# Gated linear attention, spectral mixing and a gated convolution: another way to form the next state, and an earlier place for a weight piece

## The chip, the cores and the metric

The kernel runs on one core of a Trainium2 chip. The metric is device time in microseconds (us) of one execution; three executions of the kernel before took 575.1, 575.26 and 575.69 us. The core has five engines with a queue each: PE (TensorE, matrix products; its weight loads are shown apart as PEld), DVE (VectorE), ACT (ScalarE), POOL (GpSimd) and SP (which issues the DMAs here). Each queue runs in order.

## The reference

```
# 1: gated linear attention, per batch (4), head (8), time step (768), head size 48
state = alpha[t][:, None] * state + outer(k[t], v[t])
y[t]  = q[t] @ state
# 2: spectral mixing, x = y as (4, 768, 384)
theta = x @ w_theta
zr, zi = x * cos(theta), x * sin(theta)
u = x + w_tok_r @ zr + w_tok_i @ zi          # w_tok: 768 x 768, over time
x = u + relu(u @ w_ch)
# 3: gated convolution
h = relu(x @ w_in)                           # 384 -> 1024
c = conv over time, kernel 3, of h
out = (h * sigmoid(c)) @ w_out
```

## The kernel before, in words

**Chunks.** The sequence is cut into chunks of 128 time steps, six to a batch (NC), 24 in all (NCH). Within a chunk the recurrence is done by matrix products. `a_prep` forms running products of alpha by two scans on DVE (L245, L250) and multiplies q and k by them (L259); `ftot` holds, for each of the 4 pairs of heads and each of the 2 x 48 state rows, the chunk's total decay (copied by ACT, L253), and ACT reads both scans once more to guard against overflow (the `Square` of L256, which writes into the tile that the alphas came in and reads the scan's tile, of which there is one). `a_score` makes the masked scores: matmuls into `sc`, copies by ACT to `pt` (L277), the causal mask on POOL (L278); it also turns k into `kt` (transposes L268, copy L282). `a_y` adds the chunk's own part (scores times v) and the old state's part (q times S) into `y` on PE, copies `y` to `x` on ACT (L302), and makes the next state. `a_xt` turns x (L336) and copies it to `u` (L337); `a_theta` does the sine and cosine part and splits its result into a high part `zh` (ACT cast) and a low part `zl` (DVE).

**State.** Two tiles S of 128 x 4 x 96 take turns. Rows 0 to 47 and 64 to 111 are the two heads of a pair, the third dimension has 48 columns for each; only the two diagonal blocks of 48 x 48 for a pair are non-zero. The state is kept already multiplied by the next chunk's decay, so that S for chunk c+1 is (S of c plus k^T v of c) times `ftot` of c+1. In the kernel before, PE makes `kv` for both heads of a pair at once (96 columns, of which half are not used, L308), DVE adds S and kv (L312), and POOL multiplies the two blocks by the decay (L320, twice). In the first chunk of a batch there is no old state: ACT copies the two blocks of kv (L317) and POOL multiplies.

**Token weights.** `w_tok` comes in 12 pieces of 128 x 2 x 384 words of 8 bytes (`load_tok`, `load_split`): a DMA into one of two staging buffers (STB), a decode of three DVE instructions (L116 to L118), and then, later, in `piece()`, a cast on ACT (L73) and the low part on DVE (L74), after which the staging buffer is free for another DMA. The cast is tied by an order-only edge (`behind`) to come after the latest pt, kt, x and u copies issued so far.

**Order.** A planner orders each engine's queue at build time from a simulated run; what comes earlier in the program goes first where two are ready. `a_att(b, c)` loads two chunks ahead, preps and scores one chunk ahead, then does `a_y` and `a_xt` of its own chunk. In batch 0 `piece()` follows `a_att`, in the loop of b = 0 too, for the second half of the token weights. The token mixing of batch b (`m_mix`: 18 matmuls for a chunk into `yps`) runs on PE among the attention of batch b + 1, and in batch 0 as its inputs come ready. After the four batches, parts 2 and 3 go on with PE as the busiest engine.

## Time and profile before

| | |
|---|---|
| median of three executions | 575.26 us |
| the profiled execution's own time | 576.95 us |
| its span, first to last instruction | 575.2 us |
| busy PE / PEld | 552.1 us (96%) / 523.4 us (91%) |
| busy DVE / ACT / POOL | 452.5 (79%) / 335.3 (58%) / 94.5 us (16%) |
| chain that ended last | PE 75%, DVE 13%, DMA 4%, POOL 3%, ACT 2%, issue 2% |

The span is the time between the first and the last instruction of the profiled execution; its own time has 1.75 us more around it. A table by stretch shows how long each engine was busy in it, and the clock that PE was granted as a share of full speed. A row of the timeline has the start, the duration, the engine, the line, the operation and its tiles, and in brackets how long the engine had sat idle just before and what released it.

### The profile page before, as it was taken

The page shows a single profiled execution, that of the slowest core. Times are in us where ns is not written, and L with a number is a line of the kernel's source. Part 1 is how long each engine was busy: PE and PEld are TensorE (multiplying, and loading weights), DVE is VectorE, ACT ScalarE, POOL GpSimd, SP SyncE. Part 2 cuts the span into 40 slices and gives each one's busy share as a digit, 9 for nine tenths or more (in the row PEclk, how much of TensorE's full clock was granted, in tenths as well). Part 3 has the DMA queues.
Part 4 walks back from the last instruction along what each step waited for, and adds up shares of the span by engine and source line. Part 5 has one row for each costly group of instructions (what it writes and reads, how often), then busy time and mean ns, then how long its engine had stood idle before and what let it go on. Part 6 is the DMA issues. An engine that isn't in the chain of part 4 may idle for free.

```text
span 575.2 us, 10883 instructions
## 1 busy us (share of the span) xinstructions
PE 552.1 (96%) x4371; PEld 523.4 (91%) x4371; DVE 452.5 (79%) x682; ACT 335.3 (58%) x685; POOL 94.5 (16%) x99
## 2 busy tenths in 40 slices
PE   6887988999999999999999999999999999999996
PEld 3776877887899999999999999999999999999996
DVE  8899997999866775551657989997888889798781
ACT  3576664546864467542742435557766776667571
POOL 2455415540044300350000000000000000000000
PEclk9599999999999999999999999999999999999999
DMA  8556642764034400310005333221043445536001
GB/s 326 148 180 192 206 147 73 248 215 172 15 94 138 170 2 14 95 60 2 1 2 188 113 111 111 82 83 42 15 144 136 173 138 167 193 107 229 20 30 46
DMA packets 25402, 66.59 MB, mean 116 GB/s; under 512 B 2560, under 2 KB 8704, under 8 KB 24960
## 3 DMA queue, kind: packets, MB, share of 16 engines
q1 hardware_dynamic: 25344, 65.82, 34.4%
q8 instruction: 36, 0.59, 0.4%
q14 instruction: 22, 0.18, 0.1%
HBM read 61.10 MB, written 4.72 MB: 114 GB/s over the span
## 4 chain that ended last, share of the span: by engine, by line
PE 75%; DVE 13%; DMA 4%; POOL 3%; ACT 2%; issue 2%; SPq 0%; DVEq 0%; ACTq 0%; POOLq 0%
PE yps L65 22%; PE ops L65 17%; PE hps L65 15%; PE th L65 5%; PE y L65 5%; PE cps L65 3%; PE sc L65 3%; PE kv L65 2%; DMA stage<-in_w_tok_dram 2%; POOL S L320 2%; DVE fbt L245 1%; PE xps L336 1%; DMA stage<-in_w_out_dram 1%; POOL pt L278 1%; DVE stage L117 1%
## 5 line engine op out<-in xcount | busy, mean ns | idle before, releaser
L65 PE MATMUL yps<-wtok,zh 128*128 128x384 f32 x576 | 152.7, 343 | 1.3 <-ACT zh L73 1.3
L65 PEld LDWEIGHTS yps<-wtok,zh 128*128 128x128 f32 x576 | 104.3, 189 | 4.7 <-ACT zh L73 1.6
L65 PE MATMUL hps<-x,win 128*128 128x386 f32 x576 | 107.3, 339 | 0.0
L65 PE MATMUL ops<-wout,g 128*128 128x384 f32 x576 | 107.1, 338 | 0.0
L65 PEld LDWEIGHTS hps<-x,win 128*128 128x128 f32 x576 | 102.1, 189 | 0.0
L65 PEld LDWEIGHTS ops<-wout,g 128*128 128x128 f32 x576 | 101.7, 187 | 0.0
L65 PE MATMUL yps<-wtok,zl 128*128 128x384 f32 x288 | 96.8, 340 | 0.3 <-DVE zl L74 0.3
L278 POOL TENSOR_SCALAR_AFFINE_SELECT pt<-pt 128x512 f32<-128x512 f32 x48 | 59.0, 1252 | 151.6 <-ACT pt L277 151.5
L65 PEld LDWEIGHTS yps<-wtok,zl 128*128 128x128 f32 x288 | 54.4, 189 | 1.6 <-DVE zl L74 0.6
L245 DVE TENSOR_TENSOR_SCAN fbt<-a_t,onehot 128x516 f32<-128x516 f32 x24 | 29.8, 1242 | 24.7 <-ACT a_t L256 22.9
L74 DVE TENSOR_TENSOR g<-cv,g 128x384 fp32r<-128x384 f32 x64 | 35.5, 555 | 15.0 <-ACT g L73 14.4
L550 ACT ACTIVATE cv<-cv 128x384 f32<-128x384 f32 x64 | 33.2, 522 | 22.5 <-DVE cv L547 22.5
L544 DVE SCALAR_TENSOR_TENSOR cv<-hh,cw,cv 128x383 f32<-128x383 f32 (+1 forms) x64 | 38.5, 615 | 7.3 <-ACT cv L541 6.9
L73 ACT CAST g<-cv 128x384 fp32r<-128x384 f32 x64 | 32.6, 510 | 15.3 <-DVE cv L551 13.9
L551 DVE SCALAR_TENSOR_TENSOR cv<-cv,hh 128x384 f32<-128x384 f32 x64 | 35.2, 556 | 7.7 <-ACT cv L550 5.9
L541 ACT ACTIVATE cv<-hh,cw 128x384 f32<-128x384 f32 x64 | 38.4, 615 | 4.2 <-DVE g L74 3.9
L65 PE MATMUL cps<-us,wch 128*128 128x384 f32 x216 | 40.2, 338 | 0.2 <-DVE u L495 0.2
L547 DVE SCALAR_TENSOR_TENSOR cv<-hh,cw,cv 128x384 f32<-128x384 f32 (+1 forms) x64 | 38.3, 615 | 0.6
L65 PEld LDWEIGHTS cps<-us,wch 128*128 128x128 f32 x216 | 38.1, 188 | 0.5 <-issue 0.5
L539 ACT ACTIVATE hh<-hps 128x386 f32<-128x386 f32 x64 | 31.4, 492 | 9.8 <-PE hps L65 9.6
L368 DVE TENSOR_TENSOR zf<-x,zf 128x768 f32<-128x768 f32 x24 | 23.8, 992 | 13.1 <-ACT zf L367 13.1
L259 DVE TENSOR_TENSOR qk_t<-qk_t,fbt 128x1024 f32<-128x1024 f32 x24 | 32.8, 1365 | 0.9
(90 smaller groups left out, 828.5 us busy)
## 6 DMA issues: line engine op xcount, KB each, us to landing
qk_t<-in_qka_dram SPq DMA_DIRECT2D x24, 512.0 KB, 4.6
stage<-in_w_tok_dram SPq DMA_DIRECT2D x12, 768.0 KB, 4.7
top<-in_w_tok_dram SPq DMA_DIRECT2D x12, 768.0 KB, 4.3
a_t<-in_qka_dram SPq DMA_DIRECT2D x24, 260.0 KB, 2.7
v_t<-in_v_dram SPq DMA_DIRECT2D x24, 192.0 KB, 3.8
out_dram<-ob SPq DMA_DIRECT2D x24, 192.0 KB, 1.9
stage<-in_w_in_dram SPq DMA_DIRECT2D x4, 768.0 KB, 4.4
stage<-in_w_out_dram SPq DMA_DIRECT2D x4, 768.0 KB, 4.3
```

The lines of the kernel that those rows point to most:

```text
L65: nc.tensor.matmul(o, lhsT, rhs, start=start, stop=stop, skip_group_check=True)
L73: cast = nc.scalar.copy(hi, src)
L74: lo_eng.tensor_tensor(lo, src, hi.bitcast(F32), ALU.subtract)
L245: nc.vector.tensor_tensor_scan(bf[:, AW:0:-1], at[:, AW:0:-1], of[:, AW:0:-1], 0.0, ALU.mult, ALU.add)
L259: nc.vector.tensor_tensor(q4, q4, fl.rearrange("p b (a t) -> p b a t", a=4)[:, :, :, :P], ALU.mult)
L278: nc.gpsimd.affine_select(pt, pt, [[0, NP], [1, P]], ALU.is_ge, 0.0, base=0, channel_multiplier=-1)
L539: nc.scalar.activation(hh, ps[:, :HW], AF.Relu)
L541: nc.scalar.activation(cv, hh[:, o : o + HALF], AF.Copy, scale=cw[:, f, 1:2])
L544: nc.vector.scalar_tensor_tensor(cv[:, a:HALF], hh[:, o + a - 1 : o + HALF - 1], cw[:, f, 0:1], cv[:, a:HALF], ALU.mult, ALU.add)
L547: nc.vector.scalar_tensor_tensor(cv[:, 0:e], hh[:, o + 1 : o + 1 + e], cw[:, f, 2:3], cv[:, 0:e], ALU.mult, ALU.add)
L550: nc.scalar.activation(cv, cv, AF.Tanh, scale=0.5)
L551: nc.vector.scalar_tensor_tensor(cv, cv, 1.0, hh[:, o : o + HALF], ALU.add, ALU.mult)
```

## The change

The next state is formed by other engines, in another order. POOL multiplies the old state by the decay (before kv is needed), ACT scales kv by the same decay as it reads it from PSUM (one instruction for each pair, 48 columns), and DVE adds the two, a block at a time. In the first chunk of a batch ACT writes the scaled blocks straight into the new state: eight instructions, and POOL has none. PE makes kv for each head by itself, 48 columns to a matmul, in as many matmuls as before. And `piece()` is called in `a_att` between the scores of the next chunk and `a_y` of this one, in place of after `a_att`.

```diff
-                    kv = ps_a.tile([P, NP, 2 * D], F32, tag="a", name="kv")
+                    kv = ps_a.tile([P, NP, D], F32, tag="a", name="kv")
                     for p in range(NP):
-                        for t in halves:
-                            mm(kv[t, p, :], kt[:, p, t], vt[:, p * 96 : p * 96 + 96], p == 0, True)
+                        for j, t in enumerate(halves):
+                            h = 2 * p + j
+                            mm(kv[t, p, :], kt[:, p, t], vt[:, h * D : (h + 1) * D], p == 0, True)
                     nft = prep[ci + 1][2]
+                    blocks = [(slice(64 * j, 64 * j + D), slice(j * D, (j + 1) * D)) for j in range(2)]
                     if c > 0:
-                        tt = att.tile([P, NP, 2 * D], F32, tag="tst", name="tst", bufs=1)
-                        nc.vector.tensor_tensor(tt[:112], Sp[:112], kv[:112], ALU.add)
+                        tt = att.tile([P, 2, NP, D], F32, tag="tst", name="tst", bufs=1)
+                        for r, e in blocks:
+                            nc.gpsimd.tensor_tensor(
+                                tt[r, 0], Sp[r, :, e], nft[r].unsqueeze(2).to_broadcast([D, NP, D]), ALU.mult
+                            )
+                        for p in range(NP):
+                            nc.scalar.activation(tt[:112, 1, p], kv[:112, p], AF.Copy, scale=nft[:112, p : p + 1])
+                        for r, e in blocks:
+                            nc.vector.tensor_tensor(Sn[r, :, e], tt[r, 0], tt[r, 1], ALU.add)
                     else:
-                        tt = Sn
-                        for j in range(2):
-                            nc.scalar.copy(Sn[r, :, j * D : (j + 1) * D], kv[r, :, j * D : (j + 1) * D])
-                    for j in range(2):
-                        nc.gpsimd.tensor_tensor(Sn[r, ...], tt[r, ...], nft[r] broadcast, ALU.mult)
+                        for p in range(NP):
+                            for r, e in blocks:
+                                nc.scalar.activation(Sn[r, p, e], kv[r, p], AF.Copy, scale=nft[r, p : p + 1])
...
-            def a_att(b, c):
+            def a_att(b, c, between=None):
...
                     a_prep(ci + 1)
                     a_score(ci + 1)
+                if between:
+                    between()
                 a_y(ci)
                 a_xt(ci)
...
             for c in range(NC):
-                a_att(0, c)
+                a_att(0, c, None if slow or c == 0 else piece)
...
-                else:
+                elif slow:
                     piece()
                 piece = load_tok(0, c)
...
-                    a_att(b + 1, c)
+                    a_att(b + 1, c, None if slow or b > 0 or c == 0 else piece)
                     if b == 0:
-                        if c > 0:
+                        if slow and c > 0:
                             piece()
                         piece = load_tok(1, c)
```

## Rows read from the trace of the kernel before

**Rows 1.** Busy time by stretch: stretch, length, PE, PEld, DVE, ACT, POOL, PEclk, DMA, GB/s.
```profile
40.00:60.00 20.00, 16.16 (x195) 13.96 (x195) 19.42 (x24) 12.75 (x26) 13.40 (x8) 0.92 0.59 179
60.00:80.00 20.00, 20.00 (x184) 16.76 (x185) 19.48 (x23) 12.92 (x25) 4.63 (x5) 1.00 0.53 180
80.00:100.00 20.00, 16.38 (x214) 14.46 (x211) 15.80 (x21) 11.38 (x23) 10.74 (x8) 1.00 0.28 90
160.00:200.00 40.00, 40.00 (x526) 37.79 (x525) 26.77 (x32) 20.32 (x47) 18.06 (x20) 1.00 0.45 141
```

**Rows 2.** Waits of PE over the whole span: waiter, released by: us in total, times, longest.
```profile
PE y L65 <- POOL S L320: 6.0, 4, 2.3
PE yps L65 <- ACT zh L73: 1.3, 1, 1.3
```

**Rows 3.** Timeline, PE: old-state part of y, three of the four waits.
```profile
45.03 0.88 PE L65 MATMUL y<-S,qk_t 128*64 128x96 f32 x16 [1.51 <-POOL S L320]
55.62 0.88 PE L65 MATMUL y<-S,qk_t 128*64 128x96 f32 x16 [2.33 <-POOL S L320]
92.38 0.88 PE L65 MATMUL y<-S,qk_t 128*64 128x96 f32 x16 [1.96 <-POOL S L320]
```

**Rows 4.** Timeline, batch 1: first chunk's state, copied by ACT, multiplied by POOL.
```profile
83.84 5.51 POOL L278 TENSOR_SCALAR_AFFINE_SELECT pt<-pt 128x512 f32<-128x512 f32 x2 [13.23 <-ACT pt L277]
85.91 0.66 ACT L317 COPY S<-kv 48x192 f32<-48x192 f32 x2
89.32 3.01 POOL L320 TENSOR_TENSOR S<-S,ftot 48x192 f32<-48x192 f32 x2
```

**Rows 5.** Chain that ended last, in order of time: start, us, what.
```profile
154.31 1.07 PE y L65 x32
170.96 0.66 PE kv L65 x16
```

**Rows 6.** Instructions that touch S: duration ns min/median/max.
```profile
L320 POOL TENSOR_TENSOR S<-tst,ftot x32: 498/504/3965, 30.8 to 259.2; 48x192 f32<-48x192 f32 x32
L312 DVE TENSOR_TENSOR tst<-S,kv x16: 532/541/555, 29.7 to 258.0; 112x384 f32<-112x384 f32 x16
L317 ACT COPY S<-kv x8: 310/314/320, 17.6 to 230.5; 48x192 f32<-48x192 f32 x8
```

**Rows 7.** Groups of instructions by shape, 0 to 270 us: busy us, mean ns.
```profile
L253 ACT COPY ftot<-fbt 128x4 f32<-128x4 f32 x24 | 4.8, 198 | 41.3 <-DVE fbt L245 31.8 <-POOL S L320 9.5
L249 DVE RECIPROCAL starts<-fbt 128x4 f32<-128x4 f32 x24 | 4.3, 178 | 0.6
L74 DVE TENSOR_TENSOR wth<-stage,wth 128x768 fp32r<-128x768 f32 x1 | 1.0, 952 | 0.0
L74 DVE TENSOR_TENSOR wth<-stage,wth 128x384 fp32r<-128x384 f32 x1 | 0.6, 551 | 0.0
```

**Rows 8.** The page's groups: ACT with and without a scale read from a tile.
```profile
L73 ACT CAST g<-cv 128x384 fp32r<-128x384 f32 x64 | 32.6, 510 | 15.3 <-DVE cv L551 13.9
L541 ACT ACTIVATE cv<-hh,cw 128x384 f32<-128x384 f32 x64 | 38.4, 615 | 4.2 <-DVE g L74 3.9
```

**Rows 9.** Timeline, batch 0: ACT's Square and the scans of DVE behind it.
```profile
23.17 1.23 DVE L245 TENSOR_TENSOR_SCAN fbt<-a_t,onehot 128x516 f32<-128x516 f32 x1 [1.41 <-ACT a_t L256]
31.77 0.19 ACT L256 ACTIVATION_READ_ACCUMULATOR a_t<-fbt 128x1 f32 x1
32.08 1.53 DVE L245 TENSOR_TENSOR_SCAN fbt<-a_t,onehot 128x516 f32<-128x516 f32 x1
51.52 0.20 ACT L256 ACTIVATION_READ_ACCUMULATOR a_t<-fbt 128x1 f32 x1
53.47 1.21 DVE L245 TENSOR_TENSOR_SCAN fbt<-a_t,onehot 128x516 f32<-128x516 f32 x1
```

**Rows 10.** Timeline, batch 0, a later chunk: state, piece and staging buffer.
```profile
48.60 0.56 DVE L116 TENSOR_SCALAR stage<-stage 128x768 uint32<-128x768 uint32 x1 [0.41 <-DMA stage<-in_w_tok_dram]
49.45 0.48 ACT L337 COPY u<-xps 128x384 f32<-128x384 f32 x1
```

## What was predicted before the run

> **What bounds the kernel now.** The table by stretch comes first, because the change touches only the attention part (the first 265 us) and the bound there is not the same throughout. From 160 to 200 us PE is busy for the whole 40 us while DVE works 26.8 and ACT 20.3: there PE is the bound, and the next state is formed in its shadow. From 40 to 60 us PE has 16.2 of 20 us and DVE 19.4; from 60 to 80 both are full (PE 20.0, DVE 19.5); from 80 to 100 both have holes (16.4 and 15.8) [rows 1]. So the early stretch is held by DVE and by chains that pass through it, and in the late one each PE instruction saved is time saved.
>
> The waits of PE come next. Its largest is the old-state part of y waiting for POOL to write S: 6.0 us in four waits [rows 2]. The timeline has three of them: 1.51 us at 45.0 and 2.33 us at 55.6, in batch 0, and 1.96 us at 92.4, behind the first chunk of batch 1 [rows 3]; what is left over, 0.2 us, is the fourth. The instructions that touch S say why: a multiply by POOL takes 504 ns in the middle of the list and 3,965 ns at the longest [rows 6]. The reader should see that the change aims at these four waits and at the width of kv, and that the first two lie where DVE, not POOL, has no time left.
>
> **The change part by part.**
>
> *kv with 48 columns.* There are as many matmuls, half as wide. The trace has the same form in the chunk's own part of y: 32 records in 1.07 us, 33.4 ns each, against 16 records of kv in 0.66 us, 41.3 ns each [rows 5]. So a chunk's kv falls from 0.66 to 0.53 us, by 0.13 us. Fifteen chunks make kv from batch 1 on, where PE is the bound: 15 x 0.13 = 2.0 us gained. The five in batch 0 give nothing while DVE holds the pace. Bounds: nothing, if weight loads set the pace of either width, and half of 0.66, 15 x 0.33 = 5.0 us, if columns alone did. I take 2.0, since the narrow form itself is in the rows.
>
> The Trainium skill (TensorE: Matmul & The Clock Gate, section Back-to-back issue gap) gives an isolated matmul of up to 64 columns a floor of about 25 ns. By that a record of kv would fall by 16 ns rather than 8, and this term would be an estimated 3.9 us. The 33.4 ns of the trace, in a stream with a weight load for each matmul, speak for the smaller figure.
>
> *The first chunk of a batch.* Now: two copies by ACT, 0.66 us, then POOL, whose two multiplies took 3.01 us at 89.3 because they stood behind two masks of together 5.51 us [rows 4]. After: eight ACT instructions of 48 columns with the scale read from a tile, and no POOL. No row has this form. A copy of 4 columns takes 198 ns [rows 7], one of 192 columns 314 ns [rows 6], so 48 columns lie near 225 ns; a scale read from a tile adds 615 - 510 = 105 ns [rows 8]: 0.33 us each. Bounds: 0.20 (the small copy) and 0.42 (192 columns plus the scale). Eight are 2.64 us, 1.98 more than the copies (0.94 to 2.7). At 85.9 us this puts S at about 88.6 in place of 92.3, before the mask that y waits for anyway (83.84 + 5.51 = 89.35) [rows 4]. The wait of 1.96 us at 92.4 goes, and as DVE has holes there, I count it in full: with the 0.2 us of the fourth wait 2.2 us gained. What is late next is the mask on POOL, then PE's own queue.
>
> *The later chunks.* L312 on DVE (541 ns) and POOL's multiplies behind it give way to four ACT instructions (4 x 0.33 = 1.32 us, 0.8 to 1.7) and two adds of 192 columns on DVE; POOL's multiplies stay, 32 of them, but read the old S and need not wait for kv. An add costs, by the line through 551 ns (384 columns) and 952 ns (768) [rows 7], 0.35 us; two are 0.70, 0.16 more than L312. Bounds for one are 178 ns (the smallest DVE row there [rows 7]) and L312's 541: -0.2 to +0.5 us a chunk. In batches 1 to 3 PE covers this, and ACT too, with half of its time free [rows 1]. The path from kv to S was L312 and two multiplies, at least 0.54 + 2 x 0.50 = 1.54 us [rows 6], and is now 1.32 + 0.70 = 2.02 us; PE, full from 160 to 200 us with the mixing between the chunks, never waited for the old one, so I cost the 0.5 us at nothing. Without that cover it would be 12 x 0.5 = 6 us.
>
> *Batch 0, where nothing covers.* Each chunk's new ACT work stands in ACT's queue ahead of the Square, and the next scan of DVE (L245) must wait for the Square, since it overwrites the scans' tile. At 23.2 us DVE already sat 1.41 us for it; at 32.08 the scan began 0.12 us after the Square's read-out ended (31.96); at 53.47 there are 1.75 us between them [rows 9]. So the first chunk's 1.98 us can fall on DVE; I take 1.0, half, because a ready decode instruction can be planned into that hole. The second chunk's 1.32 us falls where slack is 0.1: I take 0.7, half again, as the add and the piece may go in between. The third and fourth have slack like that at 53.5, over 1.32: nothing. The last one's ACT work meets an ACT that waits for PE, nothing. The adds give 4 x 0.16 = 0.6. Sum: 2.3 us more for DVE.
>
> Two waits of 3.84 us in all leave PE in this batch [rows 3]. They are worth nothing by themselves as long as DVE has 19.4 us of work in 20: PE would then wait for a scan, a z or a piece instead.
>
> *The piece.* Cast and low part move ahead of x and u of the same chunk. In ACT's queue that frees the cast from one copy of 0.48 us (u), not more, since it stays tied behind pt and kt. Its DMA waits for the buffer that the low part frees, so the next DMA can start by up to 0.48 us sooner; DVE waited 0.41 us for such a DMA at 48.6 [rows 10]. SP's queue gets no new issue, only these earlier; the loads queued behind it move by as much. The low part of 0.95 us (the 768-column row [rows 7]) may now be planned ahead of the adds, which delays S by so much: PE has no need of S so soon. I take 0.4 us gained for one such wait, bounds 0.95 lost and 1.0 gained.
>
> Batch 0 then has DVE 1.9 us later. Part of DVE's work there (scans two chunks ahead, decodes for the second half of the weights) has time to spare, so I count half: 0.9 us lost.
>
> **Sum.** -2.0 - 2.2 + 0.9 = -3.3 us. The profiled execution goes from 576.95 to 573.65 us, its span from 575.2 to 571.9. The median of the runs, 575.26, lies 1.69 below that execution; I take the same difference: 572.0 us.
>
> **The rivals.**
>
> *PE, not DVE, sets batch 0.* Then the first two waits pay as well, and DVE's 2.3 us lie in slack. For it: PE is full from 60 to 80 us. Against it: DVE is as well [rows 1]. Time: 575.26 - 2.0 - 6.0 = 567.3 us.
>
> *ACT takes POOL's place: slower.* If the planner puts every scaled copy ahead of the Square, L245 starts late in each chunk of batch 0: 1.98 + 4 x 1.32 = 7.3 us, less the 4.2 gained, is 3.1 us slower, 578.3 us. It decides from the point at which the added ACT time exceeds the gap between Square and scan, 0.1 us in one row and 1.75 in the other [rows 9]. For it: PE, DVE and ACT hang in one loop there. Against it: ACT works 12.8 of 20 us [rows 1] and loses 9.5 us of waits of `ftot` for POOL [rows 7], which the early multiply frees.
>
> *The add comes as late as POOL did.* DVE's queue, not POOL, decides when S is ready, and the wait at 92.4 stays in another name. Then only kv's width is left, less the 0.9: 575.26 - 1.1 = 574.2, no change. Against it: DVE has holes at that place.
>
> *DVE and POOL shut each other out.* The long POOL multiplies show that POOL slows beside a busy DVE [rows 6]; L312 reads one operand from PSUM, the new adds read both from SBUF, and so can be caught in turn. If each of the eight adds of batch 0 is 0.3 us longer (as the scan that took 1.53 us in place of 1.21 [rows 9]), 2.4 us go: 574.4, no change. The Trainium skill (SBUF — State Buffer, section Who interferes with whom) states it as a rule: a DVE instruction with two SBUF inputs contends with a POOL instruction that reads SBUF. By that rule each add is at risk; the stretched multiplies agree that the two meet, and no row has an add of this kind.
>
> **How the numbers follow.** The forecast has a chance of 0.40, PE as the bound in batch 0 0.18, ACT in POOL's place 0.20, the late add 0.16, the shut-out 0.06. Less than 0.2% (1.15 us) is no change that a measurement of this kernel can tell. The forecast's own range is 569.5 to 574.5, so nearly all of it, and the first rival, are faster: with a little of the others 0.60. The two in the middle give 0.20, ACT's rival 0.20 slower. The range goes from 567.0, the first rival, to 577.8, most of ACT's.
>
> **What would show it.** kv as 16 records in about 0.53 us in the chain; no wait of PE for S at the first chunk of batch 1, and S there by ACT before the mask ends; ACT instructions of 0.33 us; in batch 0 DVE no less full, with a wait of L245 for the Square longer than 1.41 us near 23 us, and PE waiting for something else than POOL. The prediction is wrong if PE's idle time up to 100 us falls by 5 us or more, or rises at all, or if PE waits for S in the late batches.

## The result and the profile after

The kernel after takes 583.85 us (median of 4 runs, 583.21 to 586.04), the kernel before 575.48 us (4 runs) beside it: 1.0133 of the time, 95% interval 1.0098 to 1.0169, or 5.6 to 9.7 us slower. The forecast was 572.0 us, with a range of 567.0 to 577.8. A ratio below is against runs of the kernel before made beside the run in question; it need not equal the quotient of the medians, and compares better than they do.

The profiled execution has a span of 582.2 us, 7.0 more than before. PE's busy time fell by 0.9 us (551.2 against 552.1), its idle time rose by 7.9 (31.0 against 23.1), and 7.0 of this lies in the first 310 us (25.1 against 18.1). So PE has no more work; it waits more. (A busy time grows where the granted clock falls, so idle time alone is not the loss.) The first view is the table by stretch of the kernel after (stretch, length, PE, PEld, DVE, ACT, POOL, PEclk, DMA, GB/s).

```profile
40.00:60.00 20.00, 20.00 (x212) 16.63 (x211) 19.02 (x25) 16.00 (x40) 8.09 (x8) 0.97 0.57 168
60.00:80.00 20.00, 16.34 (x119) 12.92 (x118) 17.25 (x21) 10.90 (x23) 2.51 (x2) 0.83 0.58 184
80.00:100.00 20.00, 19.71 (x219) 17.08 (x219) 16.35 (x21) 14.98 (x36) 6.96 (x6) 1.00 0.28 95
100.00:120.00 20.00, 16.62 (x252) 15.25 (x249) 16.56 (x23) 11.01 (x28) 7.47 (x8) 1.00 0.54 180
120.00:160.00 40.00, 36.69 (x257) 29.91 (x258) 34.33 (x49) 23.33 (x47) 4.94 (x6) 1.00 0.40 139
160.00:200.00 40.00, 38.59 (x533) 36.17 (x533) 27.52 (x35) 28.53 (x73) 16.98 (x18) 1.00 0.36 105
```

Against [rows 1] the holes have moved. From 40 to 60 us PE is full, where it had 3.84 us of idle; from 60 to 80 it now idles 3.66 at a clock of 0.83, where it was full at 1.00. From 100 to 160 us it idles 6.7 (before: 1.25). And where PE lost time, DVE is less busy too (17.25 against 19.48 us from 60 to 80, and 50.9 against 55.8 from 100 to 160). The rows of the kernel before for these last two stretches:

```profile
100.00:120.00 20.00, 19.08 (x251) 17.34 (x247) 19.55 (x23) 10.15 (x22) 9.22 (x10) 1.00 0.68 221
120.00:160.00 40.00, 39.67 (x290) 33.06 (x290) 36.24 (x48) 28.55 (x54) 7.45 (x7) 1.00 0.37 123
```

The instructions of the new state, by tile (duration ns min/median/max, first and last start), in the kernel after:

```profile
L65 PE MATMUL kv<-v_t,kt x320: 206/222/307, 14.3 to 264.5; 128*64 128x48 f32 x160
L319 ACT ACTIVATE tst<-kv,ftot x64: 301/335/353, 28.0 to 265.5; 112x48 f32<-112x48 f32 x64
L325 ACT ACTIVATE S<-kv,ftot x32: 295/296/307, 15.9 to 239.1; 48x48 f32<-48x48 f32 x32
L321 DVE TENSOR_TENSOR S<-tst x32: 339/356/740, 31.0 to 266.3; 48x192 f32<-48x192 f32 x32
L315 POOL TENSOR_TENSOR tst<-S,ftot x32: 500/506/1415, 22.0 to 261.7; 48x192 f32<-48x192 f32 x32
```

They cost about what was forecast (0.33 us on ACT, 0.35 on DVE), and POOL's longest multiply fell from 3,965 ns [rows 6] to 1,415. Waits to 310 us (us in total, times, longest), of the kernel after and then of the kernel before:

```profile
PE xps L336 <- ACT x L302: 10.3, 4, 3.9
DVE stage L116 <- DMA stage<-in_w_tok_dram: 8.6, 6, 2.5
PE y L65 <- DVE S L321: 2.1, 3, 1.1
```
```profile
PE xps L336 <- ACT x L302: 3.7, 2, 2.2
DVE stage L116 <- DMA stage<-in_w_tok_dram: 1.0, 3, 0.4
```

The 6.0 us for POOL's S [rows 2] are gone, with 2.1 us for the add in their place. PE now waits 10.3 us for x (before: 3.7), and DVE 8.6 us for the DMAs of the token weights (before: 1.0); such a wait of DVE is called a stand below. Two of the four waits for x (3.95 us at 20.76, 2.29 us at 37.98) come before the first stand, which ends at 67.24. The longest of the others, 3.66 us, is linked with that stand. First DVE, then ACT, then PE, in the kernel after:

```profile
67.24 0.56 DVE L116 TENSOR_SCALAR stage<-stage 128x768 uint32<-128x768 uint32 x1 [0.87 <-DMA stage<-in_w_tok_dram]
67.72 1.23 DVE L250 TENSOR_TENSOR_SCAN fbt<-a_t,starts 128x516 f32<-128x516 f32 x1
68.86 0.53 DVE L364 SCALAR_TENSOR_TENSOR zf<-zf,th 128x384 f32<-128x384 f32 x1
...
69.42 0.52 ACT L365 ACTIVATE zf<-zf 128x384 f32<-128x384 f32 x1 [2.54 <-DVE zf L364]
...
70.91 1.05 ACT L277 COPY pt<-sc 128x512 f32<-128x512 f32 x2
71.85 0.84 ACT L73 CAST wtok<-stage 128x768 fp32r<-128x768 f32 x1
72.59 0.49 ACT L302 COPY x<-y 128x384 f32<-128x384 f32 x1
...
73.13 0.90 PE L336 MATMUL xps<-ident,x 128*128 128x128 f32 x3 [3.66 <-ACT x L302]
73.82 4.05 PE L65 MATMUL th<-whole,u 128*128 128x384 f32 x6
```

At 60 us the kernel after is ahead: it starts `xps` of the fifth chunk at 60.42 us, the kernel before at 61.70 (in the third and fourth chunk it was 0.9 and 1.6 us behind). Then the first decode instruction stands at the head of DVE's queue for its DMA, with the second scan and the turn of z (L364, which takes the whole turns off theta) behind it, both ready: the reciprocal that the scan needs ended at 66.37. ACT waits 2.54 us for that turn; behind it in ACT's queue are pt, the cast and x. The turn starts 2.49 us after the reciprocal's end, and only 0.87 of them are the stand: 0.48 are the decode's first instruction and 1.14 the scan, which both stand ahead of the turn now. On ACT the cast ahead of x adds 0.74. PE gets x at 73.13, though its y was made by 66.1. In the kernel before, the same queue had the scan, the turn, the other scan and the factors first, and the decode only at 70.04, without a wait. Behind the gap PE ran at the lower clock level: six matmuls of theta in 4.05 us (2.10 in the kernel before, at 71.06). The starts of `xps` follow the loss: the kernel after is 1.3 us ahead in the fifth chunk, 2.7 behind in the seventh (89.89 against 87.22) and 5.8 behind in the twelfth (134.01 against 128.19).

The chain of work that ended last, for 40 to 135 us alone, shares by line; of the kernel before, then of the kernel after:

```profile
by line: PE yps L65 16.1%; POOL S L320 9.8%; issue 8.0%; POOL pt L278 7.1%; PE th L65 6.5%; DMA stage<-in_w_tok_dram 5.9%; DVE fbt L245 5.1%; PE y L65 4.6%; DVE fbt L250 3.9%; ACT a_t L256 3.4%; DVE stage L117 3.2%; DVE stage L116 2.6%; DVE
```
```profile
by line: DMA stage<-in_w_tok_dram 30.5%; DVE qk_t L259 9.0%; DVE wtok L74 7.1%; DVE stage L117 6.4%; DVE fbt L250 6.4%; issue 5.5%; DVE zf L368 3.7%; DVE stage L116 3.4%; PE th L65 2.7%; DVE fbt L245 2.6%; ACT S L325 2.4%; PE sc L65 2.3%; P
```

POOL has left the chain (9.8% and 7.1% before), and the DMA into the staging buffer has taken it, with 30.5% against 5.9. Its pieces, 60 to 80 us, close a loop in the kernel after (start, us, what):

```profile
61.65 0.87 DVE wtok L74
62.52 0.02 issue
62.53 4.68 DMA stage<-in_w_tok_dram
67.22 0.02 issue
67.24 0.56 DVE stage L116
67.80 1.15 DVE fbt L250
...
73.56 1.32 DVE wtok L74
74.88 0.02 issue
74.89 4.64 DMA stage<-in_w_tok_dram
```

The low part frees a buffer, the DMA takes 4.7 us, the decode stands for it with the attention's work behind it, and the next low part is late by as much.

### The profile page after: what moved, and what is told of

It reads as the page before. It is cut to its first block, busy times and chain, and to the rows that moved or that the text cites. A ratio compares the mean times of both kernels' runs of the same rounds, so it can differ in the third digit from the quotient of the medians.

```text
span 582.2 us, 11014 instructions
## 1 busy us (share of the span) xinstructions
PE 551.2 (95%) x4371; PEld 520.5 (89%) x4371; DVE 455.6 (78%) x698; ACT 354.6 (61%) x773; POOL 79.0 (14%) x91
## 4 chain that ended last, share of the span: by engine, by line
PE 74%; DVE 13%; DMA 6%; ACT 4%; issue 2%; DVEq 0%; ACTq 0%
PE yps L65 20%; PE hps L65 17%; PE ops L65 17%; PE cps L65 6%; DMA stage<-in_w_tok_dram 5%; PE th L65 4%; PE y L65 4%; PE sc L65 3%; DVE qk_t L259 3%; DVE fbt L250 2%; DVE wtok L74 1%; DVE stage L117 1%; DVE fbt L245 1%; DVE zf L368 1%; PE xps L336 1%
## 5 line engine op out<-in xcount | busy, mean ns | idle before, releaser
L278 POOL TENSOR_SCALAR_AFFINE_SELECT pt<-pt 128x512 f32<-128x512 f32 x48 | 51.9, 1105 | 150.1 <-ACT pt L277 150.0
L73 ACT CAST g<-cv 128x384 fp32r<-128x384 f32 x64 | 32.6, 510 | 11.7 <-DVE cv L553 10.5
L65 PE MATMUL sc<-qk_t 48*128 48x128 f32 x384 | 32.9, 291 | 3.2 <-issue 2.0
L65 PEld LDWEIGHTS sc<-qk_t 48*128 48x128 f32 x384 | 27.8, 193 | 8.7 <-issue 6.5
```

What stands on the lines that cost most here:

```text
L65: nc.tensor.matmul(o, lhsT, rhs, start=start, stop=stop, skip_group_check=True)
L73: cast = nc.scalar.copy(hi, src)
L278: nc.gpsimd.affine_select(pt, pt, [[0, NP], [1, P]], ALU.is_ge, 0.0, base=0, channel_multiplier=-1)
```

## The experiments

The first two split the change. **The state alone**: the kernel after, with the piece behind the chunk again.

```diff
-                a_att(0, c, None if slow or c == 0 else piece)
+                a_att(0, c)
```

> The changed kernel with the piece back behind the whole chunk, so that only the next state is formed in the new way. Theory 1 (the earlier piece is the cause: its decode is planned ahead of L259 in DVE's queue and stands there until the DMA lands, 8.6 us of such waits in the changed kernel against 1.0 before, and on ACT the cast gets ahead of the copy of y): the time is that of the kernel before or less, 572 to 576 us, and DVE's waits for the token weight DMA are under 2.5 us. Theory 2 (the new state's work on ACT and DVE is the cause): 581 to 585 us as in the changed kernel.

Measured: 578.46 us, ratio 1.0040 (1.0022 to 1.0057), between the two ranges; the stands are 3.5 us, where under 2.5 was expected. In its profile PE's busy time is 3.6 us below that of the kernel before, but its idle time to 310 us is 5.0 above. By stretch, PE idles 3.6 us more before 40 us, 3.8 less from 40 to 60 (0.07 us in place of 3.84: the two waits for POOL lay there), 2.7 more from 60 to 100 and 2.5 more from 100 to 160. Before 40 us the first chunk's eight ACT instructions took 2.45 us where two copies took 0.65, and x, `xps` (22.38 against 20.67 us) and the Square came that much later. By 60 us this is made up, and the loss that stays comes behind it. There, with the piece in its old place, the turn of z was late as well: a low part (79.67) and the second scan (80.52) had gone ahead of it, though its input was ready at 78.89.

```profile
81.66 0.53 DVE L364 SCALAR_TENSOR_TENSOR zf<-zf,th 128x384 f32<-128x384 f32 x1
82.22 0.52 ACT L365 ACTIVATE zf<-zf 128x384 f32<-128x384 f32 x1 [2.45 <-DVE zf L364]
```

In the profiled execution of the kernel after, the same eight instructions did not put x off, by luck: PE reached its higher clock level earlier there (16 score matmuls from 12.60 us took 1.49 us, against 2.67 in the kernel before and in this run), kv came 1.3 us earlier than before, and `xps` started at 20.76.

**The piece alone**: the kernel before, with the new place of `piece()` and no other edit.

> The kernel before with only the piece moved ahead of y; the next state is formed in the old way. Theory 1 (earlier piece): 580 to 585 us, DVE's waits for the token weight DMA over 5 us. Theory 2 (state): 574 to 577 us. If the two parts only hurt together: both this and the other part alone stay at 573 to 578 us.

Measured: 585.52 us, ratio 1.0166 (1.0144 to 1.0188): more than the whole change. It issues the same instructions as the kernel before, so only an order can cost. PE idles 5.1 us more to 310 us, and is busy 4.9 us longer over the span (557.0 against 552.1): about half of the loss is matmuls at the lower clock level. The timeline of this run, DVE, ACT and PE:

```profile
78.24 0.56 DVE L116 TENSOR_SCALAR stage<-stage 128x768 uint32<-128x768 uint32 x1 [1.92 <-DMA stage<-in_w_tok_dram]
78.72 0.55 DVE L364 SCALAR_TENSOR_TENSOR zf<-zf,th 128x384 f32<-128x384 f32 x1
...
79.30 0.52 ACT L365 ACTIVATE zf<-zf 128x384 f32<-128x384 f32 x1 [2.69 <-DVE zf L364]
...
85.12 2.29 PE L65 MATMUL yps<-wtok,zh 128*128 128x384 f32 x6 [3.52 <-ACT zh L73]
```

It is the same figure: decode at the queue's head, turn of z behind it, ACT idle, PE idle, and then six matmuls in 2.29 us, at the lower level (six took 1.34 us in a run below). DVE's stands for these DMAs sum to 7.9 us, and PE's waits for POOL's S rose from 6.0 to 8.3.

**The decode later, and the piece later.** Two tries to keep the new place without the harm. In the first the decode is issued with the cast and tied behind the factors of the scores; in the second `between()` comes behind `a_y`.

```diff
+                if lazy:
+                    behind(first, ("qk",))
...
+                a_y(ci)
                 if between:
                     between()
-                a_y(ci)
```

> The changed kernel, but the three decode instructions of a piece are issued together with its cast and low part, with an order edge that puts the first of them behind the latest L259; the DMA is issued where it was. That takes away what makes L259 stand behind a DMA. Theory 1: DVE's waits for the token weight DMA fall under 2 us and the time by 3 to 8 us, to 576 to 581 us; what is left of the loss is the cast ahead of the copy of y. Theory 2: no change, 582 to 586 us.

> The changed kernel with the piece between the chunk's y (and its next state) and the transposes of x, one step later. In ACT's queue the copy of y is then ahead of the cast, but in DVE's queue one or two decodes of the second chunk row still stand early. Theory 1: PE's waits for the copy of y fall from 10.3 to 4 to 7 us, the waits for DMA to 2 to 5 us, the time to 574 to 580 us. Theory 2: 581 to 585 us.

Measured: 585.71 us (1.0170, 1.0142 to 1.0199) and 586.32 us (1.0180, 1.0158 to 1.0203). Both missed. The first cut the stands from 8.6 to 3.0 us and gained nothing: its decode still stood 0.96 us ahead of a scan and a turn (PE then waited 3.04 us for x at 75.60), and elsewhere decode and low part together went ahead of the adds (PE waited 2.38 us for S at 104.02). In the second x came ahead of the cast, as wanted, but L116 stood ahead of the scan and the turn at 69.23 as before, and PE waited 3.29 us for x: here the late turn alone was enough for such a wait, without the cast ahead of x.

**Where the piece costs.** The new place in batch 0 alone, and in batch 1 alone, both with the new state.

> The changed kernel with the piece moved ahead of y only in the first loop (pieces of the first half of the token weights, batch 0); in batch 1 it follows the chunk as before. Theory 1a (in batch 0 the decode stands ahead of L250 and L364 of the next chunk, the copy of y on ACT comes late, PE stops for over 3 us near 73 us and its granted clock falls after the stop): a wait of PE for the copy of y of over 3 us at 70 to 76 us, PEclk 0.80 to 0.95 in the 20 us around it, 580 to 585 us. If instead batch 1 carries the loss: 576 to 579.5 us, as with the state alone.

> The changed kernel with the piece moved ahead of y only in batch 1 (pieces of the second half), batch 0 as with the state alone. Theory 1b (in batch 1 the decode stands ahead of L259 and waits there for its DMA, 2.5 + 1.0 + 1.9 us in the changed kernel): waits of DVE for that DMA over 4 us, PE waits for S and for the scores near 110 to 125 us, no low clock after 60 us, 580 to 583 us, that is 2 to 5 us over the state alone. If batch 0 carries the loss: 576 to 579.5 us.

Measured: 582.83 us (1.0095, 1.0066 to 1.0125) and 581.46 us (1.0088, 1.0063 to 1.0112). Above the state alone (1.0040) these are 0.0055 and 0.0048, and 0.0040 + 0.0055 + 0.0048 = 0.0143, near the 0.0133 of all together. The sum is rough: by the medians (575.30 us for the kernel before beside these runs) the two parts would be 0.0085 and 0.0061. Each batch costs. That each does so by its own stands is not shown: with the new place in batch 0 alone, the longest stand (2.79 us of 6.3) ends at 109.33, in batch 1.

**Inside the state.** The first chunk as it was (ACT copies, POOL multiplies), the rest new, the piece in its old place; and, in the kernel before, only kv narrow.

```diff
-                        for p in range(NP):
-                            for r, e in blocks:
-                                nc.scalar.activation(Sn[r, p, e], kv[r, p], AF.Copy, scale=nft[r, p : p + 1])
+                        for r, e in blocks:
+                            nc.scalar.copy(Sn[r, :, e], kv[r])
...
```

> The new state alone (piece as before), but in the first chunk of a batch in the old way: ACT copies, POOL multiplies. What it tells: whether the eight ACT instructions of the first chunk make the state part slower. If they do (ACT's work ahead of the Square and of the copy of y in batch 0, xps 1.7 us later at 22 us): 574 to 577 us, and xps near 20.7 us. If the adds on DVE and the four ACT instructions of later chunks do: 577.5 to 580 us.

> The kernel before with kv of 48 columns in place of 96 and nothing else: DVE still adds once, over 384 columns with kv read twice, and POOL multiplies. By the working of the prediction 2.0 us less than before, 573 to 574.3 us, with kv at 0.53 us a chunk in place of 0.66. Rival: DVE is full to 134 us and PE waits for it there, so that only the ten chunks of batches 2 and 3 pay: 1.0 to 1.4 us less, 574 to 575 us; or the new plan around it costs more than it gives, 576 us or more.

Measured: 577.90 us (1.0018, 0.9995 to 1.0042), and 575.36 us (0.9989, 0.9967 to 1.0012). With the old first chunk `xps` is back at 20.60 us, as expected if the eight instructions cost, but the time lies where it was expected if they do not; the intervals of this run and of the state alone overlap, so the first chunk's share is not settled. The narrow kv does save PE time, in the timeline of this run against that of the kernel before:

```profile
240.78 0.62 PE L65 MATMUL kv<-v_t,kt 128*64 128x48 f32 x16
241.33 0.45 PE L65 MATMUL yps<-wtok,zh 128*128 128x384 f32 x1
```
```profile
242.96 0.83 PE L65 MATMUL kv<-v_t,kt 128*64 128x96 f32 x16
243.72 0.45 PE L65 MATMUL yps<-wtok,zh 128*128 128x384 f32 x1
```

From the start of kv to the start of what follows it is 0.55 us in place of 0.76, 0.21 a chunk, and PE is busy 546.5 us in place of 552.1. Yet PE idles 2.7 us more, and over the runs the gain is 0.6 us, with an interval that holds zero.

**Is it the work of the decode, or its stand?** In both kernels, once with two of the three decode instructions left out for the 12 pieces, once with no DMA for a piece after the second (the two buffers in use are decoded again).

```diff
+            if short:
+                return
             nc.vector.scalar_tensor_tensor(fb, hi, 0xC0000000, fb, ALU.bitwise_and, ALU.bitwise_or)
...
+            if piece_load and len(held) == 2:
+                st = held[turns.pop(0)]
```

> The changed kernel with only the first of the three decode instructions of each token weight piece (L117 and L118 left out for the 12 pieces, so the token weights are not what they should be): 12 x 1.9 us less work on DVE before 135 us, DMAs and waits for them as they were. To be read against the same cut in the kernel before. Theory A (DVE is full, and the earlier piece puts 3.4 us of decode and low part ahead of the scans, z and the adds that PE waits for): with DVE relieved the two kernels come within 3 us of each other, both at 564 to 572 us. Theory B (the decode stands in DVE's queue until a late DMA lands): the changed kernel stays 6 to 9 us slower than the other with the same cut.

> The kernel before with the same cut (L117 and L118 left out for the 12 pieces, so the token weights are not what they should be): the other half of the pair. If DVE holds PE in batches 0 and 1: 564 to 571 us. If PE's own work holds it: 573 to 576 us.

> The changed kernel with the DMAs of the last 10 of the 12 token weight pieces left out: their decodes read the two staging buffers that the first two filled (the token weights are then not what they should be). The work on DVE and ACT stays whole, no decode can wait for a DMA. To be read against the same cut in the kernel before. Theory B (late DMA): the two come within 3 us of each other, the changed kernel at 574 to 578 us. Theory A (order of the work on a full DVE): the changed kernel stays 5 to 9 us slower than the other.

> The kernel before with the same DMAs left out: the other half of that pair. Its waits for these DMAs were 1.0 us in all, so 573 to 576 us by either theory, unless the decodes that no longer wait are planned earlier, ahead of what PE waits for: then, by theory A, 577 to 583 us even here.

| | kernel after | kernel before |
|---|---|---|
| as it is | 583.85 us, 1.0133 | 575.48 us |
| short decode | 581.85, 1.0096 (1.0063 to 1.0128) | 565.00, 0.9804 (0.9774 to 0.9834) |
| no DMA for pieces | 583.64, 1.0123 (1.0093 to 1.0154) | 583.16, 1.0121 (1.0086 to 1.0156) |
| both cuts | 570.07, 0.9918 (0.9888 to 0.9948) | 565.97, 0.9831 (0.9805 to 0.9856) |

With a short decode the kernel after gains 2 us and the kernel before 11: that DVE was merely full, which should have given both the same, falls. In the kernel after the stands grow to 15.6 us, as DVE with less work comes to the DMAs sooner. Without the DMAs it is no faster either, so the stand alone isn't it: the decode then goes ahead of the scan as 2.5 us of work, and PE waited 2.23 us for z at 87.99. And the *old* kernel without the DMAs becomes as slow as the new one, and the planner now puts decodes ahead of scan and turn there too. At 65.15 us, where L116 goes ahead of the turn, nothing is lost yet (it starts `xps` of the seventh chunk at 83.59, the kernel before at 87.22). At 75.70 and 77.31 two L116, and at 78.22 and 79.18 two L117, stand ahead of the second scan, which starts 5.2 us behind the first (76.17, 81.36; in the kernel before 1.8). From 80 to 100 us PE has 15.21 us at a clock of 0.74 (before: 16.38 at 1.00), and the eighth chunk's `xps` is late (98.82 against 96.76). A new theory follows: work and stand are two halves of one cost, and either is enough to do harm from that place.

**Both cuts at once** (the last row of the table), and, the other way round, **one decode put ahead by hand in the kernel before**, with two order-only edges:

```diff
+                marks["dec"] = first
...
+                if ci == NC + 1:
+                    behind(scan2, ("dec",))
...
+                if ci == NC - 2 and not slow:
+                    behind(turn_off, ("dec",))
```

> The kernel after, with both cuts at once: 12 token weight pieces are decoded by one of the three DVE instructions (about 2 us of DVE less for each), and from the third piece on there is no new DMA, the two staging buffers in use are decoded again. The output is not the reference's. Theory (a decode planned ahead of the scan, the z turn and the scores' factors costs PE in two ways, as work of 2.5 us and as a stand for its DMA, and either is enough): with both gone the order no longer matters, and this kernel lies within 3 us of the old kernel with the same cuts, both near 565. Rival (the state's new way, or ACT's order, holds PE and the decode only happens to stand there): more than 5 us above the old kernel with the same cuts.

> The kernel before with the same two cuts (one decode instruction for each of 12 pieces, no DMA for a piece after the second). The output is not the reference's. Theory: near 565, as with the short decode alone, and within 3 us of the kernel after with both cuts; its waits on DMAs fall below the 3.2 us that the short decode left. Rival: the pair stays more than 5 us apart.

> The kernel before with one place in DVE's queue changed by hand: the second scan for chunk 7 and the turn of z of chunk 4 are issued behind the first decode instruction of piece (0,5). No instruction is added or taken away. Theory (the decode's place in the queue is the cause): 577.5 to 582, with that scan and that turn late, a wait of PE over 2.5 us for x or z between 65 and 95 us, and a granted clock under 1.0 in the stretch behind it. Rival (the piece costs by its cast or its low part, or the planner's other orders): 575 to 576.5, no such wait.

The pair is 4.1 us apart in the medians: between the 3 of the theory and the 5 of its rival. The table by stretch of the two, after and then before with both cuts, says where:

```profile
0.00:20.00 20.00, 12.93 (x101) 8.69 (x101) 15.61 (x21) 7.54 (x17) 3.69 (x12) 0.82 0.78 277
20.00:40.00 20.00, 13.16 (x181) 11.08 (x182) 13.65 (x18) 14.39 (x35) 7.99 (x10) 0.83 0.49 149
40.00:310.00 270.00, 267.65 (x2655) 247.75 (x2655) 191.04 (x255) 174.30 (x394) 66.07 (x69) 0.99 0.27 81
```
```profile
0.00:20.00 20.00, 13.45 (x101) 9.21 (x101) 15.47 (x21) 6.85 (x14) 4.30 (x14) 0.83 0.78 276
20.00:40.00 20.00, 16.23 (x199) 13.35 (x199) 15.34 (x19) 14.80 (x31) 10.48 (x11) 0.91 0.52 150
40.00:310.00 270.00, 268.46 (x2664) 249.31 (x2663) 187.27 (x244) 156.49 (x314) 65.50 (x75) 1.00 0.27 83
```

Behind 40 us they idle 2.35 and 1.54 us, against 10.4 in the kernel after with the short decode alone: what the piece cost is gone. The casts and low parts are still in their new place there, so these cost little by themselves, at least beside a DVE that has this much less to do. Taking the DMAs away from a short decode gave the kernel after 11.8 us (581.85 to 570.07) and the kernel before nothing (565.00, 565.97): in the kernel after the stand costs. Before 40 us the new one idles 3.6 us more (13.9 against 10.3), as the state alone did in the first experiment.

The hand-made order gave 578.21 us, 1.0054 (1.0031 to 1.0076), 1.8 to 4.4 us slower: the time that was expected. DVE and PE in this run:

```profile
68.44 0.56 DVE L116 TENSOR_SCALAR stage<-stage 128x768 uint32<-128x768 uint32 x1 [0.43 <-DMA stage<-in_w_tok_dram]
68.91 1.66 DVE L253 TENSOR_TENSOR_SCAN fbt<-a_t,starts 128x516 f32<-128x516 f32 x1
...
82.48 1.34 PE L65 MATMUL yps<-wtok,zh 128*128 128x384 f32 x6 [2.29 <-ACT zh L73]
```

The scan stands behind the decode, which stands for its DMA. But the trace does not show the loss at this place. The second edge changed nothing, as the turn of z of chunk 4 came behind this decode in the kernel before too (76.86 against 70.04). PE starts `xps` of the sixth and seventh chunks at 70.10 and 85.09 us, 0.6 and 2.1 us ahead of the kernel before, and of the ninth level with it (103.70, 103.68). Its wait for z of 2.29 us (over 2.5 was expected) is 1.0 us longer than in the kernel before [rows 2], and ahead of the turn for it (78.42) stand a low part (76.44) and a second scan (77.28), not the decode. The clock from 80 to 100 us is 0.91 in place of 1.00. Behind 310 us PE has as much left to do as before (260.2 and 260.1 us), and the profiled span is 1.1 us longer by idle time at the end. The planner moved other instructions with the edge, so the run shows that an order can cost this much, and not that this place does.

**Is DVE's time the currency?** The short decode took some 11 us off the kernel before. So the low part of the 12 pieces went to POOL, in the kernel before, with the new state but the old first chunk and the old place of the piece, and in the kernel after.

```diff
-                cast = split(out_hi, out_lo, full, nc.vector)
+                lo_eng = nc.gpsimd if tag == "st" and scale is None and not slow else nc.vector
+                cast = split(out_hi, out_lo, full, lo_eng)
```

> The kernel before with the low part of the 12 token weight pieces (0.95 us each on DVE, 11.4 us in all) computed by GpSimd. Theory (until about 134 us DVE has no time left, and time taken from it comes back): the short decode took some 25 us off DVE and gave 10.3, so 11.4 us less should give 4 to 5: 570 to 572. Rival (GpSimd, which needs 0.5 us for 192 columns and up to 4 beside DVE, now holds the masks and the state's multiply up behind a subtraction of 768 columns): PE's waits for S rise above 6.0 us, 577 or more.

> The new state from the second chunk of a batch on, with the old first chunk and the piece in its old place (577.9 us), with the low part of the 12 pieces on GpSimd. Theory: as GpSimd's multiply no longer waits for kv, it does not stand between kv and y, so this version bears the low part better than the old one: 571 to 574, below the old state with the same edit or equal to it. Rival (DVE's two adds behind GpSimd's multiply wait as long): as far above the old state with the same edit as without it, by 2 us or more.

> The kernel after with the low part of the 12 pieces on GpSimd. Theory (the decode's place in the queue costs, and it stays where it is): DVE has 11.4 us less, but the decode still stands for its DMA, so it stays above the other two with this edit, 574 to 580. Rival (the low part between scores and y is what costs): level with the kernel that has the new state alone and the same edit, within 1.5 us.

Measured: 588.57 us (1.0219, 1.0172 to 1.0266), 587.13 (1.0193, 1.0158 to 1.0228) and 587.84 (1.0214, 1.0174 to 1.0254). All three are some 12 us slower than the kernel before. In the first the rival's number came, but not for its reason: PE's waits for S fell to 4.2 us. The first one's groups, 0 to 150 us (busy us, mean ns):

```profile
L74 POOL TENSOR_TENSOR wtok<-stage,wtok 128x768 fp32r<-128x768 f32 x12 | 25.3, 2111 | 10.9 <-ACT wtok L73 10.3
L260 DVE TENSOR_TENSOR qk_t<-qk_t,fbt 128x1024 f32<-128x1024 f32 x15 | 24.2, 1616 | 0.5
L246 DVE TENSOR_TENSOR_SCAN fbt<-a_t,onehot 128x516 f32<-128x516 f32 x15 | 22.5, 1501 | 5.8 <-ACT a_t L257 4.2 <-DMA a_t<-in_qka_dram 1.5
```

POOL took 25.3 us for the twelve. DVE was rid of 11.7 us, but the factors took 1,616 ns each in place of 1,319 (24.2 us against 19.8) and the first scan 1,501 in place of 1,248 (22.5 against 18.7): over 8 us of the 11.7 went into these two lines. And the stands came: DVE stood 9.9 us for the DMAs of the pieces in the first run (1.0 in the kernel before), 6.1 and 5.1 in the others. In the first run the next DMA was issued as POOL's low part ended (61.03 us after a low part of 58.36 + 2.65, for one), so a slower low part means a later DMA. That speaks for the stand, but the two harms are mixed here. DVE's time was not freed, so this test says nothing on whether freed time would pay, and as all three came out level it doesn't tell the decode's place from the low part's either.

## Why the prediction was wrong

**The piece** is the step that failed most. It was forecast at 0.4 us gained, with bounds of -0.95 and +1.0; it costs 9.6 us on the old state (1.0166) and some 5.4 on the new one (1.0133 less 1.0040). The prediction asked by how much the cast and the DMA move, let the low part delay only the adds, and called the rest nothing. What it left out is that the planner sets each queue's order from a simulated run, so that an earlier cast means an earlier free buffer, an earlier DMA, and an earlier place for the next decode, ahead of the second scan, the turn of z and the factors. There an instruction with two kinds of harm stands: its DMA has not landed (8.6 us of stands), and it is 2.5 us of work ahead of what PE waits for. Shown for this: the place of the piece alone, with the same instructions, costs 1.0166; with a short decode, taking the DMAs away gives the kernel after 11.8 us and the kernel before nothing; and with both halves cut the two kernels idle the same behind 40 us to within 0.8 us. Not shown: that nothing else in the new orders costs. Putting one such place into the old kernel by hand gave the time that was expected, but its trace does not have the loss at that place. The turn of z is late in the state alone too, behind a low part and a scan, so the decode is not the only instruction that the planner puts ahead of it. The cast ahead of x (0.74 us at the place shown) and the low part ahead of the adds (waits of 2.1 us in three) are small where they can be read. A third staging buffer, which might take the stand away by itself, was not tried.

**The bound from batch 1 on.** That PE is the bound "from batch 1 on" was read from 160 to 200 us [rows 1]. The rows between were not asked: from 100 to 120 us the kernel before has DVE at 19.55 of 20 us, and at 36.24 of 40 from 120 to 160, with the second half of the weights being decoded, beside a PE at 19.08 and 39.67. So the harm of the piece in batch 1 (0.0048) had no cover, and *kv* did not pay as forecast: the saving was mis-sized on the low side (0.21 us a chunk, not 0.13, as the wide form took 47 ns a matmul and not 41.3), but alone it gave 0.6 us (-0.7 to 1.9) and not 2.0. The Trainium skill (TensorE: Matmul & The Clock Gate, section Back-to-back issue gap) puts the floor of an isolated matmul of up to 64 columns at about 25 ns. The trace, with a weight load for each matmul, has 0.55 us for 16, 34 ns each, and agrees with the row that the prediction took.

**The first chunk, the later chunks and POOL's waits** went as worked out in size: 2.45 us for the eight instructions (2.64 forecast), 335 and 356 ns for the others, and all four waits, 6.0 us [rows 2], went. In batch 0 they counted too, as the first rival said: in the state alone PE idles 0.07 us from 40 to 60 us in place of 3.84, and `xps` goes from 3.0 us behind in the third chunk to 0.4 in the fifth. The waits for S that are left lie in batch 1 and none in the late batches. **Batch 0** was the term with the wrong weight: 0.9 us lost was forecast, and the state alone, which should have been about 3 us faster without the piece, is 1.3 to 3.3 us slower. Before 40 us its PE idles 3.6 us more, where ACT's eight instructions put off x directly. The prediction followed them to DVE by way of the Square (the scan waited 2.52 us in the state alone, as forecast over 1.41) and not to x, which stands behind them on ACT and which PE waits for. That is made up by 60 us. The 5.2 us more from 60 to 160 us are in no term of the prediction, which held the new state's work covered from batch 1 on. The late turn at 81.66 is one place of them; for the rest, and for the first chunk's share, the cause stays open.

**The rivals.** "ACT takes POOL's place" named the right side and a chain that is there, but in the whole change ACT was not what failed: its queue waited for DVE's turn. That its 578.3 us is near the 578.46 of the state alone is luck, as the loss there lies elsewhere. "The add comes as late" is there with 2.1 us. "DVE and POOL shut each other out" is not seen in the adds (356 ns in the middle, 740 at most, where 2 x 350 was forecast for a pair), and is plain where POOL subtracts 768 columns. **What would show it:** PE's idle time up to 100 us rose by 0.2 us (16.8 to 17.0), which is the sign named there for a wrong prediction; more of it lay behind, from 100 to 160 us (5.4 us). And a part lies in the clock: of some 4.2 us that kv saved (20 x 0.21) PE's busy time shows 0.9 (5.6 in the kernel with only kv narrow), as the stretch behind the gap at 73.13, to 79.24 us, ran at half clock (6.1 us, an estimated 3 us of it lost). Over the whole span the mean clock is as before (0.981 and 0.982): it is 0.89 in place of 0.83 to 60 us, where PE had 13 us of idle time in both, and 0.94 in place of 1.00 from 60 to 120 us.

## What to carry to other kernels

Before moving a step in a kernel whose queues a planner orders, list what the step frees, and where the next instruction that waits for a DMA will then stand: while DVE stood at such an instruction, ready work behind it waited, and so did ACT and PE for that work. And when a change lets a planner make a new order, look at all the new queues: the state alone, which moved no piece, had its turn of z late as well. Read the bound in each stretch where a saving is to be paid, not in the clearest one. Cut both halves of a suspected cost (work and wait) before taking a failed single cut as an acquittal. And where a cost is put in by hand, see in the trace that the time is lost at that place; the total alone came out right here for a reason that stays open.

## What was not expected of the hardware

- POOL beside DVE: with POOL's twelve subtractions of 768 columns (2.11 us each) in the stretch, DVE's 1,024-column multiply went from 1,319 to 1,616 ns and its scan from 1,248 to 1,501. The Trainium skill (SBUF — State Buffer, section Who interferes with whom) has the rule that a DVE instruction with two SBUF inputs contends with a POOL instruction that reads SBUF; these rows agree and give its price here.
- Some gaps of PE were followed by matmuls at the lower of the two clock levels: 3.66 us by six of theta in 4.05 us, 3.52 and 2.23 us by six of the mixing in 2.29 us. In the hand-made order the six behind a gap of 2.29 us took 1.34 us, and the 16 of kv behind them 1.41, where they take 0.83. Not every gap was: with only kv narrow, PE sat idle 2.45 us at 66.69, and the clock stayed at 1.00.
- POOL's multiply took 3,965 ns at its longest, and 1,415 where it runs ahead of kv, with the same 500 ns at its shortest. That its new place among DVE's work is the reason was not tested.
